# One core, deltanet and a multiplicative FFN: the hand-written list of 1706 steps put in another order

## The chip, the core and the metric

The kernel runs on one core of one Trainium2 chip. The metric is the device time of one execution in microseconds (us). TensorE is called PE here (its weight loads PEld), VectorE DVE, ScalarE ACT, GpSimd POOL and SyncE SP. SP issues every DMA of this kernel.

## The reference

Two blocks are joined. The first is a delta-rule recurrence over 768 positions for 4 batches of 8 heads, head size 48; the second multiplies two projections of its output and applies two further matrices:

```python
k_n = k / (np.linalg.norm(k, axis=-1, keepdims=True) + 1e-06)
for t in range(S):
    y[:, :, t] = np.einsum('bhd,bhde->bhe', q[:, :, t], state)
    v_old = np.einsum('bhde,bhd->bhe', state, kt)
    state = state + bt[..., None, None] * np.einsum('bhd,bhe->bhde', kt, vt - v_old)
...
a = x @ w1          # x: 3072 tokens x 384, from y
b = x @ w2          # w1, w2: 384 x 1024
h = a * b @ w3      # w3: 1024 x 1024
out = h @ w_out     # w_out: 1024 x 384
```

The four weights come as 64-bit floats; everything is computed in float32.

## The kernel before

The 768 positions are cut into 12 chunks of 64 (numbers 0 to 11), and two chunks make a pair (0 to 5). In a chunk the recurrence is solved in closed form, so that only a short chain runs from chunk to chunk. Two matrices are folded on the chip: w3·w_out becomes one matrix of 1024 x 384, so the second block is two products, an element-wise product and one more product. From pair 1 on, these products are done with fewer multiplications (sums of blocks on POOL and DVE, then 20 products per half instead of 24).

The work is written as generators, one for each part, and a **step** is what a generator does up to its next `yield`. The parts that matter below, by their letters in the list (a letter, then the chunk, pair or column block):

- `P`: one piece of a weight: a DMA into one of 5 `raw` buffers (L829), two activations on ACT (L837, L840), a shift on DVE (L842), an add on POOL (L844). `P0` to `P7` are w_out, `P8` to `P23` are w3 (two for each of 8 blocks of columns), `P24` to `P35` w1 and w2.
- `t`: four transposes of a w3 piece on PE (L880) and a copy out of PSUM (L204); `f`: one block of the fold in two halves of four products each on PE (L895), and a copy (L204).
- `k`, `q`, `v`, `p`: loads (L269, L280, L297; a `p` load is 8 DMAs). `K`, `Q` (chunks 0 and 1): transposes on PE (L404) and four copies (L204); `d` (the later chunks): four stream transposes on DVE (L390).
- `N`: norms of a pair, a chain of small DVE instructions. `s`: scores of a chunk on PE in two halves (L433, L439), each with a DVE product (L445) and an ACT copy (L457) with a POOL mask (L459).
- `u` (L492): copies that lay two chunks out for the inversion; `V`: the inversion of a pair on DVE, one transpose (L508) and 31 dependent pairs of instructions (L530 and L535, or L541 and L546).
- `e`: the corner of the inverse, copies (L589), a transpose on DVE (L599), and two sets of products on PE (L616) with ACT behind them (L641, L661).
- `c`: the chain of a chunk: three sets of products on PE (L687), each followed by one DVE instruction (L718, L727, L749) that the next set reads. `y`: the chunk's outputs on PE (L786), and copies on ACT (L805).
- `b`, `a`: the first products of pair 0 (L915). `m` (L1117): the products of a later pair, two halves `m10`, `m11` and so on, with adds on DVE (L1148), copies on ACT (L1145) and sums on POOL (L200). `S`, `G`, `W`, `T`: sums of blocks. `o` (L1199): the last products, `x`: results and stores.
- `warm+3` (L194): three products of 128x512 whose result nobody reads. `zp`, `zd`: memsets.

`ORDER` is a string of 1706 step names. The kernel calls the steps in that order, and `in_text_order` then ties every instruction to the one before it on its engine, so the string fixes the order of each of the five engines and of SP's DMA queue. Nothing is moved by a planner. A step's name can carry a mark: with `'`, what the step does by `put` (a copy out of PSUM) goes to the other of ACT and DVE, and what it does by `alone` (a sum of blocks) goes from POOL to DVE. Buffers are given out in turn as the steps are called: 5 `raw` buffers, 3 of `KQ`, 2 of `X`, 4 PSUM banks `ps_f`, 2 double banks `ps_w`, 10 slabs. An instruction waits where its inputs, or the last readers of the buffer it writes, are late; all behind it on its engine wait with it.

In order of time the list holds: loads, `K`, `Q` and scores of chunks 0 and 1 while the first weight pieces are converted; the inversion `V0` on DVE beside the folds on PE; corners and chains of chunks 0 and 1 with the last folds; the first products of pair 0 (`b`, `a`) beside the chunks 2 and 3; then four stages, from `oA0` to `oA4`, in each of which PE does the last products of one pair and the first products of the next, with the chain of two more chunks between them; and a tail of pair 5 alone.

Of the kernel before, what the change touches and what calls it, by code (L numbers as in the profile page):

```python
# [39 lines left out]
warm+3 P11 beta P2 P0 P11 P11 P11 P2 beta P3 k0 K0 P0 beta P0 P0 K0' K0 P6 P6 k1 K1 zd zd zd P2 g0 P2 P9 P3  # L40
q0 K0 K0 g0 g0 g0 g0 g0 P6 P9 g0 g0 K1 P9 P3 K1 P16 K1 q1 Q0 P10 Q0' N0 K1' P6 P16 P16 P3 Q0 Q0 Q0
P12 P13 P10 s0 N0 s0 P9 P5 s0 Q1 P10 P12 Q1' P16 zp zp P12 Q1' Q1 s0 Q1' P13 P8 p2 P5 P10 t3 s0 P13
P13 s0 s0 P1 P12 u0 u0 s1 s1 s1 s1 s1 s1 P7 P4 t2 t2' t3' u0 t5 t4 P5 t5' u1 u1 u1 V0 P8 P5 V0 P8 f1
P8 V0 t1 t1 t4 t0 t8 P17 d2 zp zp zp zp zp V0 V0 V0 V0 P14 k2 P1 P1 P1 t0 N0 t8 P4 P15 V0 P7 V0 V0
V0 P7 P17 V0 P4 V0 V0 V0 P17 P7 P4 P17 f2 f0 f2 f1 V0 s1 P14 d2 V0 V0 V0 k3 P14 P15 f2 V0 s0 g1 f0
f1 g1 P14 g1 t6 t9 P19 P18 P19 f0 t9 v0 V0 V0 g1 V0 P15 V0 P19 g1 P15 P19 zp t6 P18 P23 P22 v1 f4 f4
t7 t11 t7 V0 V0 V0 t11 g1 g1 P22 P23 f3 V0 P18 V0 V0 V0 V0 g1 P26 n0 P18 t10 V0 P23 V0 P22 V0 P20
t10 N1 n0 f3 P26 f5 f5 f3 e0 N1 e0 e0 e0 e0 p2 P20 P23 P22 d2 d2 P20 e1 e0 s2 f4 p3 P21 p3 P24 P25
e0 e0 P20 n1 t12 t15 P26 f5' s2 s2 d3 c0 c0 e1 t14 s2 e1 t14 t12 t15' P21 y0 s2 s2 d3 c0 f7 y0 P26
d3 P21 P21 d3 e1 u2 u2 u2 s1 n1 e1 c0 e1 s3 s3 s3 s3 s3 s3 y0 P27 t13 P29 c1 c1 t13' e1 P24 f6 u3 u3  # L50
u3 V1 V1 V1 V1 V1 P24 V1 V1 V1 P28 P24 e1 c1 c1 P25 P27 V1 P27 V1 P29 f7 p4 P32 y1 f7 f6 y1 P25 V1
V1 V1 V1 V1 V1 y1 P28 P25 P28 P27 b0 b0 v2 P30 P31 P28 f6 d4 V1 P29 P29 zp V1 V1 V1 P32 b3 b1 b2 b1
b3 b2 b7 d4 V1 V1 P32 V1 V1 V1 V1 b7 b4 a07 c1 a04 a07 a04 b4 a02 a00 a01 P30 a05 a02 V1 V1 V1 V1 V1
V1 V1 V1 V1 a00 n2 n2 P32 a01 P31 P30 P31 a05 a03 b5 e2 e2 e2 N1 a03 P31 P33 a06 c1 k4 p4 e2 P35 P34
k5 c2 P30 e2 d4 c2 P33 b5 d4 a00 b3 e3 g2 b3 p5 e2 a06 e2 P33 a00 g2 g2 g2 P33 b2 a03 e3 e2 P34 e3
c2 a03 c2 P35 P34 g2 P35 a02 a02 g2 b2 y2 b0 d5 e3 b0 d5 a01 g2 s4 P34 W y2 v3 P35 p5 g2 a01 N2 N2
b6 a06 b6 T T W T b6 b4 W a06 e3 n3 W s4 s4 s4 s4 d5 s4 d5 a04 e3 s4 b7 b6 b4 b7 s5 s5 s5 s5 s5 T s5
u4 v4 b5 a05 W W n3 n4 e3 s5 b5 a04 W' W S0 u5 V2 e3 c2 N2 V2 c2 V2 a07 c3 b1 a05 c3 b1 V2 V2 c3 c3
V2 a07 V2 V2 V2 V2 V2 oA0 V2 V2 y3 S0 S0' W W S0 S0 S0 n4 S0 xA0 oA0 oD0 W p6 S0 S0 S0 S0 y3 S0 S0
S0 y3 S0 xA0 oB0 oC0 V2 V2 V2 V2 V2 G1 V2 xB0 oB0 S0 G1 G1 G1 G1 c3 xA0 m10 d6 V2 V2 V2 V2 V2 xB0  # L60
xC0 oC0 xD0 m10 m10 G1 G1 G1' m10 m10 m10 m10 k6 d6 xC0 V2 V2 W xC0 V2 p6 V2 xD0 xC0 V2 W V2 m10 W
# [1341 lines left out]
```

## Time and profile before

| | |
|---|---|
| three runs | 546.81 us (median), 544.82 to 550.54 |
| profiled execution | 541.17 us, of which the core's span is 539.5 us |
| profiled execution below the median | 5.64 us, 1.0% |
| mean granted TensorE clock | 0.978 |
| PE, PEld busy | 513.8 us (95%), 431.6 us (80%) |
| DVE, ACT, POOL busy | 403.2 us, 221.5 us, 274.7 us |
| DMA | 52.66 MB, mean 98 GB/s |

In the profile's lists a row names source line, engine, operation and tiles (what is written `<-` what is read), its count, and then the busy time and the mean duration in ns. The chain of waits follows the end of the program back to what released each step.

### The profile page before, as it was taken

How to read it: one execution, taken by the hardware profiler on the slowest of the kernel's cores; microseconds unless marked ns; L12 is line 12 of the kernel's file. 1: busy time of each engine (PE TensorE's matmuls, PEld its weight loads, DVE VectorE, ACT ScalarE, POOL GpSimd, SP SyncE). 2: the span in 40 equal slices, each digit the busy share in tenths (PEclk: the TensorE clock that was granted, in tenths of full speed). 3: DMA queues.
4: the chain of work that ended last, by engine and by line, in shares of the span. 5: the costliest groups of instructions: out<-in, count | busy, mean ns of one | idle time of the engine just before them, and what ended most of it. 6: DMA issues, size and time to landing. Idle time of an engine off the chain costs nothing.

```text
span 539.5 us, 19915 instructions
## 1 busy us (share of the span) xinstructions
PE 513.8 (95%) x8466; PEld 431.6 (80%) x8466; DVE 403.2 (75%) x880; ACT 221.5 (41%) x453; POOL 274.7 (51%) x296
## 2 busy tenths in 40 slices
PE   6679998999999999999999999999999999999997
PEld 3555567688888988889988889878899788997886
DVE  2689986898667997869987799887879845536562
ACT  3787586747523133532134333245321342312210
POOL 4575763344889996066932258361368302051150
PEclk7599998999999999999999999999999999999999
DMA  8979974767554264654444561644314320010001
GB/s 222 239 202 237 239 112 114 154 163 151 98 84 81 60 139 65 104 108 78 103 102 61 82 114 49 137 80 56 53 52 108 76 40 4 17 51 8 2 1 60
DMA packets 197593, 52.66 MB, mean 98 GB/s; under 512 B 184576, under 2 KB 191872, under 8 KB 197504
## 3 DMA queue, kind: packets, MB, share of 16 engines
q1 hardware_dynamic: 197504, 51.38, 46.1%
q8 instruction: 67, 1.10, 0.9%
q14 instruction: 22, 0.18, 0.1%
HBM read 41.25 MB, written 8.91 MB: 93 GB/s over the span
## 4 chain that ended last, share of the span: by engine, by line
PE 65%; DVE 14%; SPq 7%; DMA 6%; ACT 3%; issue 3%; POOL 1%; DVEq 0%; ACTq 0%; POOLq 0%
PE ps_f L1117 26%; PE ps_f L1199 20%; PE ps_w L687 5%; SPq L297 4%; PE ps_f L895 3%; PE ps_w L786 3%; DVE tb L530 3%; DVE ps_w L535 3%; PE ps_f L915 2%; DVE KQ L390 2%; PE ps_w L616 2%; DMA raw<-in_moe_w_dram 2%; DMA perm<-in_q_dram 1%; PE ps_w L433 1%; SPq L269 1%
## 5 line engine op out<-in xcount | busy, mean ns | idle before, releaser
L200 POOL TENSOR_TENSOR ab<-ab 128x512 f32<-128x512 f32 (+1 forms) x57 | 65.5, 1167 | 67.5 <-DVE ab L1148 33.7
L1199 PE MATMUL ps_f<-w,ab 128*128 128x192 f32 x376 | 65.1, 327 | 0.0
L1117 PE MATMUL ps_f<-xT,w1s 128*128 128x256 f32 x240 | 63.4, 388 | 0.1
L1117 PE MATMUL ps_f<-xT,w2s 128*128 128x256 f32 x240 | 61.7, 387 | 1.4 <-DVE x_room L1148 1.0
L1199 PEld LDWEIGHTS ps_f<-w,ab 128*128 128x128 f32 x376 | 61.9, 190 | 0.7
L1148 DVE TENSOR_TENSOR ab<-ab,ps_f 128x512 f32<-128x512 f32 x70 | 47.6, 682 | 17.1 <-PE ps_f L1117 15.4
L1117 PEld LDWEIGHTS ps_f<-xT,w1s 128*128 128x128 f32 x240 | 43.5, 189 | 9.6 <-ACT x_room L1145 1.8
L1117 PEld LDWEIGHTS ps_f<-xT,w2s 128*128 128x128 f32 x240 | 43.6, 189 | 9.3 <-DVE x_room L1148 1.7
L459 POOL TENSOR_TENSOR PT<-PT,smask 128x512 f32<-128x512 f32 x20 | 25.4, 1276 | 44.9 <-ACT PT L457 44.7
L1199 PE MATMUL ps_f<-room,ab 128*128 128x192 f32 x272 | 47.2, 329 | 0.0
L546 DVE TENSOR_TENSOR ps_w<-ps_w,tb 128x31 f32<-128x31 f32 (+15 forms) x124 | 43.3, 349 | 4.5
L895 PE MATMUL ps_f<-w2s,w3T 128*128 128x384 f32 x128 | 43.8, 492 | 1.5 <-POOL w2s L844 1.0
L1199 PEld LDWEIGHTS ps_f<-room,ab 128*128 128x128 f32 x272 | 44.2, 190 | 0.5
L541 DVE TENSOR_TENSOR tb<-ps_w,Ub 128x31 f32<-128x31 f32 (+15 forms) x124 | 41.8, 337 | 3.4 <-DMA Ub<-Ud 0.3
L805 ACT COPY xT<-ps_w 48x256 f32<-48x256 f32 x96 | 30.6, 366 | 33.4 <-PE ps_w L786 32.9
L200 POOL TENSOR_TENSOR xT<-xT 128x256 f32<-128x256 f32 x44 | 31.9, 740 | 20.6 <-DVE xT L200 14.7
L1117 PE MATMUL ps_f<-xT,room 128*128 128x256 f32 x160 | 39.9, 381 | 0.0
L895 PEld LDWEIGHTS ps_f<-w2s,w3T 128*128 128x128 f32 x128 | 23.4, 190 | 17.3 <-POOL w2s L844 2.4
L1148 DVE TENSOR_TENSOR x_room<-x_room,ps_f 128x512 f32<-128x512 f32 x40 | 27.2, 679 | 11.1 <-PE ps_f L1117 10.0
L1145 ACT COPY x_room<-ps_f 128x512 f32<-128x512 f32 x20 | 11.7, 586 | 55.6 <-PE ps_f L1117 45.3
L1117 PEld LDWEIGHTS ps_f<-xT,room 128*128 128x128 f32 x160 | 30.1, 190 | 4.1
L1145 ACT COPY ab<-ps_f 128x512 f32<-128x512 f32 x20 | 11.7, 586 | 49.7 <-PE ps_f L1117 49.6
(196 smaller groups left out, 1078.5 us busy)
## 6 DMA issues: line engine op xcount, KB each, us to landing
raw<-in_moe_w_dram SPq DMA_DIRECT2D x16, 512.0 KB, 5.8
ktok<-in_k_dram SPq DMA_DIRECT2D x48, 96.0 KB, 3.4
vtok<-in_v_dram SPq DMA_DIRECT2D x24, 192.0 KB, 4.2
raw<-in_moe_w_dram SPq DMA_DIRECT2D x24, 192.0 KB, 4.3
out_dram<-osb SPq DMA_DIRECT2D x46, 96.0 KB, 1.7
raw<-in_moe_w_out_dram SPq DMA_DIRECT2D x8, 384.0 KB, 4.2
perm<-in_k_dram SPq DMA_DIRECT2D x40, 64.0 KB, 3.0
perm<-in_q_dram SPq DMA_DIRECT2D x32, 64.0 KB, 2.6
```

The source lines that it names most:

```text
L200: (dve if other else pool).tensor_tensor(out=out, in0=x, in1=y, op=op)
L297: sync.dma_start(out=dst[quarter(2 * e + j), :, :, tb, 0:nd].rearrange("t b a d -> t (b a) d"), in_=src.rearrange("b (a e) t d -> e (b a) ...
L459: pool.tensor_tensor(out=PT, in0=PT, in1=smask[:].unsqueeze(1).to_broadcast([P, H, C]), op=ALU.mult)
L541: dve.tensor_tensor(out=tv, in0=V[:, 0 : s + 1, s : s + 1].to_broadcast([P, s + 1, n]), in1=U[:, s, s + 1 : BS].unsqueeze(1).to_broadcast( ...
L546: dve.tensor_tensor(out=o, in0=o, in1=tv, op=ALU.subtract)
L687: pe.matmul(out(ps, r, h, z), lhsT=lhs(r, h, z), rhs=rhs(r, h, z), start=True, stop=True,)
L805: act.copy(out=xT[f, cc, p:NP:2, b : b + NR, :].rearrange("p a r t -> p r a t"), in_=pyv[f, z, b : b + NR],)
L895: pe.matmul(ps[:, 0:DM], lhsT=w3Ts[jc, kc // 4][:, kc % 4 * P : kc % 4 * P + P], rhs=wo[:, kc], start=(i == 0), stop=(i == KF - 1),)
L1117: pe.matmul(ps[:, n * g : n * g + n].rearrange("p (b c t) -> p b c t", b=HB, c=2), lhsT=product_weights(i, 2 * r + g), rhs=of[i], start=na ...
L1145: act.copy(out=t, in_=cell(what[1]))
L1148: dve.tensor_tensor(out=t, in0=t, in1=cell(what[2]), op=op)
L1199: pe.matmul(ps[b][:, b, :], lhsT=block(u, HF * f + i, z)[:, P * b : P * b + P], rhs=ws_[w][:, i], start=first and i == 0 and (b == 0 or n ...
```

## The change

The string `ORDER` is replaced as a whole by another order of the same steps. Of the marks, 55 steps carry `'` where 46 did; `warm+3` is there once in both. The program that results has the same instructions but for the engine of a few copies and sums: 12 of the 16 copies of `K` and `Q` are on ACT where 8 were, and some ten sums of blocks on DVE that were on POOL. Line numbers of the changed kernel are 47 higher, since the string is laid out in more lines. All else is the same text. The first lines of each string:

```diff
-warm+3 P11 beta P2 P0 P11 P11 P11 P2 beta P3 k0 K0 P0 beta P0 P0 K0' K0 P6 P6 k1 K1 zd zd zd P2 g0 P2 P9 P3
...
+P3 P3 P3 P3 zp zp zp zp zp zd k0 g0 g0 K0 K0 K0
+K0' K0 g0 zp zp zp g0 beta P9 zp P9 k1 zd g0 g0 g0
...
```

**The opening.** On SP, from the start of the program, before; `ktok0` and `ktok1` are chunks 0 and 1 of k, `X` is q, `raw` a weight piece:

```order
1 L829 DMA raw_115<-in_moe_w3_dram 128x1024
2 L1283 DMA xT0_78<-in_beta_dram 16x12x64 x2
3 L829 DMA raw_119<-in_moe_w_out_dram 128x768
4 L829 DMA raw_121<-in_moe_w_out_dram 128x768
5 L829 DMA raw_143<-in_moe_w_out_dram 128x768
6 L269 DMA ktok0_98<-in_k_dram 64x8x48 x4
7 L829 DMA raw_191<-in_moe_w_out_dram 128x768
8 L269 DMA ktok1_99<-in_k_dram 64x8x48 x4
9 L829 DMA raw_242<-in_moe_w3_dram 128x1024
10 L280 DMA X_246<-in_q_dram 64x16x48 x2
11 L829 DMA raw_269<-in_moe_w3_dram 128x1024
12 L280 DMA X_272<-in_q_dram 64x16x48 x2
```

The same queue now:

```order
1 L876 DMA raw_111<-in_moe_w_out_dram 128x768
2 L316 DMA ktok0_98<-in_k_dram 64x8x48 x4
3 L1330 DMA xT0_78<-in_beta_dram 16x12x64 x2
4 L876 DMA raw_178<-in_moe_w3_dram 128x1024
5 L316 DMA ktok1_99<-in_k_dram 64x8x48 x4
6 L876 DMA raw_195<-in_moe_w3_dram 128x1024
7 L327 DMA X_251<-in_q_dram 64x16x48 x2
8 L876 DMA raw_254<-in_moe_w3_dram 128x1024
9 L876 DMA raw_336<-in_moe_w3_dram 128x1024
10 L876 DMA raw_342<-in_moe_w3_dram 128x1024
11 L876 DMA raw_353<-in_moe_w3_dram 128x1024
12 L327 DMA X_421<-in_q_dram 64x16x48 x2
```

One weight piece instead of four stands ahead of the first load of k, and the first load of q moves up from place 10 to 7. On DVE, where the inversion `V0` begins (`Ub` is its transposed input, L508; `tb` its first pair; `w3T` are copies of transposed w3, the first of which the first fold reads; `w2s` holds pieces of w_out), before:

```order
45 L445 TENSOR_TENSOR U0_103<-ps_w_516,wt_376 128x512
46 L204 COPY w3T_551<-ps_f_546 128x512
47 L204 COPY w3T_553<-ps_f_448 128x512
48 L842 TENSOR_SCALAR w2s_108<-w2s_108 128x384
49 L204 COPY w3T_567<-ps_f_556 128x512
50 L508 STREAM_TRANSPOSE Ub_572<-xT1_79 128x1024
51 L842 TENSOR_SCALAR w3_574<-w3_574 128x512
52 L390 STREAM_TRANSPOSE KQ_609<-perm0_95 128x8x64
53 L530 TENSOR_TENSOR tb_616<-ps_w_578,Ub_572 128x31
```

The same place now:

```order
40 L889 TENSOR_SCALAR w3_513<-w3_513 128x512
41 L492 TENSOR_TENSOR U0_103<-ps_w_485,wt_321 128x512
42 L492 TENSOR_TENSOR U0_103<-ps_w_535,wt_321 128x512
43 L555 STREAM_TRANSPOSE Ub_572<-xT1_79 128x1024
44 L889 TENSOR_SCALAR w2s_108<-w2s_108 128x384 x2
45 L251 COPY w3T_600<-ps_f_577 128x512
46 L577 TENSOR_TENSOR tb_612<-ps_w_588,Ub_572 128x31
```

The three copies of `w3T` stood ahead of the inversion's transpose; now the last that the first fold needs stands behind it. `warm+3` is no longer PE's first work but stands between the last scores of chunk 1 and the last transposes ahead of the first fold.

**The corners and chains of chunks 0 and 1.** On ACT, before; L589 are the corners' copies, `late0` (L641) is what the second set of products of chunk 0's corner reads, `w34` a fold's result, `w3` and `raw` a weight piece:

```order
83 L589 COPY TT0_94<-Ub_572 128x16x32
84 L589 COPY TT0_94<-Ub_572 32x16x32
85 L837 ACTIVATE w3_977<-raw_883 128x512
86 L840 ACTIVATE raw_883<-raw_883 128x512
87 L589 COPY TT0_94<-Ub_572 128x16x32
88 L641 COPY late0_105<-ps_w_936 32x2x8x32 x2
89 L204 COPY w34_109<-ps_f_799 128x384
90 L661 ACTIVATE TT0_94<-ps_w_1042 32x2x8x32 x2
91 L589 COPY TT0_94<-Ub_572 32x16x32
```

And now:

```order
84 L636 COPY TT0_94<-Ub_572 128x16x32
85 L636 COPY TT0_94<-Ub_572 32x16x32
86 L636 COPY TT0_94<-Ub_572 128x16x32
87 L251 COPY w34_109<-ps_f_855 128x384
88 L884 ACTIVATE w3_990<-raw_869 128x512
89 L887 ACTIVATE raw_869<-raw_869 128x512
90 L636 COPY TT0_94<-Ub_572 32x16x32
91 L688 COPY late0_105<-ps_w_954 32x2x8x32 x2
92 L708 ACTIVATE TT0_94<-ps_w_1035 32x2x8x32 x2
```

The copy of a fold's result and the second L589 copy of chunk 1 now stand ahead of `late0`. On PE a little later, before (L895 is half a fold, L616 the first set of chunk 1's corner, L433 and L439 the scores of chunk 3, L687 the first set of chunk 1's chain):

```order
243 L895 MATMUL ps_f_1242<-w2s_108,w3T_1163 128x384 x4
244 L616 MATMUL ps_w_1269<-T110_104,U0_103 33x32 x32
245 L433 MATMUL ps_w_1306<-KQ_1094 64x128 x2
...
260 L439 MATMUL ps_w_1334<-KQ_1094 64x64 x4
261 L880 MATMUL ps_f_1372<-ident_83,w3_1169 128x128 x4
262 L687 MATMUL ps_w_1382<-S_1302,KQ_199 64x48 x32
263 L616 MATMUL ps_w_1418<-TT0_94,late0_105 33x32 x2
```

And now (L833 is chunk 0's output):

```order
243 L663 MATMUL ps_w_1213<-T110_104,U0_103 33x32 x32
244 L833 MATMUL ps_w_1254<-PT_390,X_1115 48x64 x32
245 L942 MATMUL ps_f_1311<-w2s_108,w3T_1117 128x384 x4
246 L734 MATMUL ps_w_1318<-S_1203,KQ_199 64x48 x32
247 L480 MATMUL ps_w_1352<-KQ_998 64x128 x2
...
262 L486 MATMUL ps_w_1380<-KQ_998 64x64 x4
263 L663 MATMUL ps_w_1415<-TT0_94,late0_105 33x32 x2
```

The chain's first set moved ahead of the scores of chunk 3, and now follows half a fold.

**A handover in the stage of pair 3.** On DVE, from the norms of pair 5 on, before; L390 are the transposes of chunk 11, L1148 the adds behind the products `m31`, L445 the scores of chunk 10, L749 the chain of chunk 8:

```order
683 L370 TENSOR_TENSOR wt_5579<-wt_5579,nt_5480 128x32
684 L1148 TENSOR_TENSOR ab_5260<-ab_5260,ps_f_5078 128x512
685 L1148 TENSOR_TENSOR late0_105<-late0_105,ps_f_5085 128x512
686 L390 STREAM_TRANSPOSE KQ_5594<-perm0_95 128x8x64 x2
687 L1148 TENSOR_TENSOR x_room0_97<-x_room0_97,ps_f_5159 128x512
688 L1148 TENSOR_TENSOR ab_5467<-ab_5467,ps_f_5085 128x512
689 L445 TENSOR_TENSOR U0_103<-ps_w_5613,wt_5579 128x512
690 L749 TENSOR_TENSOR S_5676<-S_5232,ps_w_5639 112x768
```

And now (L646 is the transpose of the corner of chunk 9):

```order
675 L417 TENSOR_TENSOR wt_5451<-wt_5451,nt_5429 128x32
676 L437 STREAM_TRANSPOSE KQ_5579<-perm0_95 128x8x64 x2
677 L1195 TENSOR_TENSOR ab_5332<-ab_5332,ps_f_5068 128x512
678 L1195 TENSOR_TENSOR late0_105<-late0_105,ps_f_5079 128x512
679 L796 TENSOR_TENSOR S_5592<-S_5211,ps_w_5464 112x768
680 L646 STREAM_TRANSPOSE T110_104<-TT0_94 128x512
681 L1195 TENSOR_TENSOR x_room0_97<-x_room0_97,ps_f_5124 128x512
```

The two transposes stand ahead of two adds of `m31` that they stood behind, and a chain step and a corner's transpose stand ahead of the third. On SP the loads of chunk 11's k (L297) stand ahead of the eight corner loads (L578) of chunk 9 that they stood behind.

More of the change, by code (lines that the diff above doesn't have):

```diff
@@ L45 @@
[L45 to L49, printed above, removed]
@@ L99 @@
+o5 x5 S5 S5' S5 S5' o5 x5 x5 S5 S5' o5 o5 x5 o5 o5
 x5 x5 x5 x5 x5 x5 x5 x5 x5 x5
```

156 lines of the change are left out of this document (103 added, 53 removed).

## The prediction

> **What bounds the kernel now.** I read the page first, then the busy times by stretch of time, then what PE waited for, then the chain of waits. The page says who is busy and which engine the chain of waits runs through:
>
> ```profile
> span 539.5 us, 19915 instructions
> PE 513.8 (95%) x8466; PEld 431.6 (80%) x8466; DVE 403.2 (75%) x880; ACT 221.5 (41%) x453; POOL 274.7 (51%) x296
> PE 65%; DVE 14%; SPq 7%; DMA 6%; ACT 3%; issue 3%; POOL 1%; DVEq 0%; ACTq 0%; POOLq 0%
> q8 instruction: 67, 1.10, 0.9%
> ```
>
> PE is busy 95% of the span. An order can only give back what PE does not use, so the question is where that lies. By stretch (length, then busy us and count of PE, PEld, DVE, ACT, POOL, then the granted clock):
>
> ```profile
> 8.00:28.50 20.50, 12.57 (x305) 10.53 (x306) 12.99 (x35) 10.78 (x23) 10.25 (x12) 0.50 1.01 242
> 28.50:37.00 8.50, 6.25 (x160) 5.13 (x159) 6.84 (x12) 7.91 (x13) 6.95 (x6) 1.00 0.75 162
> 37.00:75.00 38.00, 36.05 (x132) 21.13 (x133) 35.46 (x100) 28.43 (x53) 24.29 (x30) 1.00 0.90 203
> 75.00:108.50 33.50, 30.29 (x945) 23.15 (x945) 24.33 (x53) 24.28 (x45) 14.99 (x15) 0.95 0.67 139
> 108.50:168.40 59.90, 59.16 (x1153) 50.01 (x1151) 44.65 (x105) 30.51 (x67) 41.60 (x42) 1.00 0.64 125
> 168.40:460.00 291.60, 289.50 (x5257) 251.72 (x5251) 237.56 (x517) 100.43 (x219) 153.17 (x163) 1.00 0.41 78
> 460.00:539.50 79.50, 74.79 (x512) 67.41 (x510) 40.56 (x62) 15.30 (x32) 20.39 (x18) 1.00 0.07 24
> ```
>
> The reader is to see five limits. To 37 us PE waits for loads and for ACT, at half clock up to 28.5 us. From 37 to 75 us the folds fill PE (36.05 of 38.00) and the inversion fills DVE (35.46). From 75 to 108.5 us PE shows 30.29 busy of 33.50, with 945 small products. From 108.5 to 460 us PE idles only 0.74 and 2.10 us. The tail waits for its last results. What PE waited for in the whole run is short:
>
> ```profile
> PE ps_f L404 <- DMA ktok<-in_k_dram: 4.4, 4, 2.7
> PE ps_f L404 <- DMA X<-in_q_dram: 3.1, 2, 1.6
> PE ps_w L687 <- issue: 2.2, 2, 1.5
> PE ps_f L1117 <- DVE x_room L1148: 1.0, 2, 0.8
> PE ps_f L895 <- POOL w2s L844: 1.0, 2, 0.7
> PE ps_f L880 <- POOL w L844: 0.8, 2, 0.6
> ```
>
> The Trainium skill, in "Perfetto Trace Analysis", section "Identifying the Most-Contended Engine", calls the matmuls' busy share a bad measure and asks for the weight loads' share; here that is 80% against 95%. So a stretch with PE "busy" can still be slow, and I look at the pace of its products below.
>
> **Term A, the opening up to 75 us: +1.0.** The rows for it are the instructions around 37 us, and the durations of what ACT and DVE do ahead of it:
>
> ```profile
> 37.04 2.20 PE L895 MATMUL ps_f<-w2s,w3T 128*128 128x384 f32 x6 [0.53 <-DVE w3T L204]
> 38.73 0.67 ACT L837 ACTIVATE w<-raw 128x512 f32<-128x512 f32 x1
> 38.87 1.25 DVE L508 STREAM_TRANSPOSE Ub<-xT 128x1024 f32<-128x1024 f32 x1 [0.36 <-POOL xT L492]
> raw<-in_moe_w_out_dram SPq DMA_DIRECT2D x8, 384.0 KB, 4.2
> L837 ACT ACTIVATE w<-raw 128x512 f32<-128x512 f32 x16 | 10.9, 681 | 7.5 <-DMA raw<-in_moe_w_dram 4.8 <-PE ps_f L895 2.6
> L840 ACT ACTIVATE raw<-raw 128x384 uint32<-128x384 uint32 x8 | 4.4, 545 | 0.0
> L204 ACT COPY KQ<-ps_f 48x512 f32<-48x512 f32 x8 | 4.6, 580 | 4.5 <-PE ps_f L404 4.3
> L492 ACT COPY xT<-U 96x512 f32<-96x512 f32 x4 | 4.3, 1084 | 1.0 <-DVE U L445 1.0
> L842 DVE TENSOR_SCALAR w2s<-w2s 128x384 uint32<-128x384 uint32 x8 | 4.0, 497 | 0.9 <-ACT w2s L837 0.9
> L204 DVE COPY w3T<-ps_f 128x512 f32<-128x512 f32 x5 | 3.3, 681 | 0.0
> ```
>
> Before, the first fold starts at 37.04 us; the last `u1` copy on ACT ends at 38.73 us, and DVE's transpose of V0 follows. Up to that copy's end ACT does 12 conversions of 128x512 (0.68 us), 10 of 128x384 (0.545), 8 copies of K and Q (0.58), 3 of PT (the same price), 4 of L492 (1.09) and 0.8 us of small ones: 25.1 us. After, it is 14, 6, 12, 3 and 4, two copies of w3T at KQ's price and 1.4 us of small ones: 28.4 us, 3.3 more. But it starts sooner and waits less. Before, ACT's first conversion starts at about 4 us, so some 9.5 us until 38.73 were waiting. The two loads that PE waited 4.4 + 3.1 us for now stand ahead of all but one to three weight pieces, so I leave 9.5 - 7.5 = 2.0 us. The first piece is issued first, at 0.8 us, and takes 4.2 to land: 5.0 + 28.4 + 2.0 = 35.4 us, so V0 begins 3.4 us sooner. The first fold, though, now stands behind V0's transpose on DVE: 1.25, two shifts of 0.497, the copy of 0.681, and three handovers of about 0.2: 35.4 + 3.5 = 38.9 us, 1.9 later. Behind it PE has the same 36.05 us of folds and transposes, and two waits for pieces (1.0 and 0.8) that a later start shortens; I give back half of them, 0.9. So A = +1.0, at 75 us. Bounds: with no waiting on ACT and both piece waits gone, -1.0; with 9.5 us of waiting kept, the start moves 7.5 us, +8.5. I stay near the lower end because the loads' places in the queue are sure. Twelve copies of K and Q on ACT instead of 8 free 4 x 0.68 us of DVE, which waits there anyway: nothing. The sums that move from POOL to DVE (about ten) lie where DVE idles 54 us of 291.6: nothing by themselves; their lateness is in term D.
>
> **Term B, 75 to 108.5 us: -1.5.** Here the chain has stops named issue, in which PE waits for nothing that the profile shows:
>
> ```profile
> 80.29 1.51 issue
> 84.34 0.57 issue
> 90.98 0.32 issue
> 94.58 0.67 issue
> 255.60 1.06 PE ps_w L687 x57
> 81.80:95.25 13.45, 12.21 (x382) 0.87 0.48 118
> L204 ACT COPY w<-ps_f 128x384 f32<-128x384 f32 x7 | 3.3, 477 | 1.8 <-PE ps_f L895 1.8
> L589 ACT COPY TT<-Ub 32x512 f32<-32x512 f32 x4 | 4.4, 1094 | 0.0
> ```
>
> Between the stops at 80.29 and 94.58 PE does 382 products in 13.45 us, 35 ns each; elsewhere 57 of the same small kind take 1.06 us, 19 ns each. PE's 2 x 8466 instructions over 67 fetched packets make 253 a packet: blocks of instructions are used up in the small products faster than they come. After, the first set of chunk 1's chain stands behind half a fold, whose four products use up 8 instructions, and no longer behind 48 products of scores; the last three stops (1.56 us) should go. Against it, on ACT the copy behind `late0` and a corner's copy move ahead of it: 0.477 + 1.094 = 1.57 us, and PE's next set of the corner waits for it; the first stop (1.51) lies within that wait, so +0.06 is left. B = -1.5. Bounds: all four stops gone and the copies hidden, -3.1; stops kept beside the copies, +1.6. The Trainium skill, in "Runtime: NRT & Kernel Launch", section "Instruction fetch mechanics", has PE's instructions come in 16 KiB blocks of 256 and a crossing mostly hidden. The packets agree (1.10 MB over 67 is 16.4 KB), the stops do not. By that rule the stops have another cause and stay, B would be +0.1 and the sum +2.6.
>
> **Term C, 108.5 to 168.4 us: 0.** PE idles 0.74 us there; the first products of pair 0 cover the chain in both orders.
>
> **Term D, the four stages to 460 us: +1.5.** A set of the chain or an add of `m` on DVE (0.682) is late for PE when PE's own work since its releaser is shorter:
>
> ```profile
> L1148 DVE TENSOR_TENSOR ab<-ab,ps_f 128x512 f32<-128x512 f32 x70 | 47.6, 682 | 17.1 <-PE ps_f L1117 15.4
> 377.37 3.07 DMA perm<-in_q_dram
> 382.71 0.33 PE L433 MATMUL ps_w<-KQ 48*64 48x128 f32 x2 [0.36 <-ACT PT L457]
> ```
>
> With these rows' durations laid along both orders, I count 13 handovers in the first three stages that are short by over 0.3 us before, and 25 after (an estimate by hand: chunk 6's corner to its chain, chunk 9's likewise, chunk 8's corner, and in the stage of pair 3 the transposes of chunk 11 ahead of two adds of m31). PE's idle time before is 2.10 us, 0.16 for each of the 13. Twelve more at 0.16: +1.9. Against it, chunk 11's k is now loaded ahead of chunk 9's corner; the 0.36 us that PE waits at 382.7 behind its late transfer should go. D = +1.5. Bounds: every one of the twelve costs a whole DVE add, +8.2; all of the 2.10 goes, -2.1. I take the low price because most of the 13 cost nothing now.
>
> **Term E, the tail: 0.** Three sums move to DVE, which is idle half of it.
>
> **Sum**: +1.0 - 1.5 + 0 + 1.5 + 0 = +1.0. The profiled execution took 541.17 us (span 539.5 and 1.7 around it), so it would take 542.2; the median of the runs is 546.81, so 547.8 on its scale. About 1% is what a measurement of this kernel can tell from no change.
>
> **The rivals.**
> - Faster: the opening's loads leave ACT without waits (A at -1.0), the fold hides the blocks (B at -3.1), and the earlier transfers take all of PE's idle time in the stages (D at -2.1): -6.2, 540.6 us. For it: V0 begins sooner, and three stops stand in the chain. Against: 28.4 us of ACT work, and 25 short handovers for 13.
> - Slower: the DVE handovers of stages 1 to 3 cost what they are short by. Place: DVE, ahead of the adds of `m`, above all chunk 11's transposes, which must wait for the outputs of chunk 8 to leave their KQ buffer. Price: 12 x 0.682 = 8.2 for 1.9, so +7.3, 554.1 us. It decides from about 0.55 us each. Against: 0.16 each now.
> - The clock: PE's unread products have left the start, and the folds begin at half clock. Before, half clock held from 8.0 to 28.5 us with PE 61% busy, full clock came with 74%. Two halves of a fold twice as slow: by the row below 8 products of 0.32 us, +2.6, so 550.4 us. For it, less work at the very start; against, the three unread products (2.42 us with a fourth) now stand straight ahead of the folds.
>
> ```profile
> 67.30 7.74 PE ps_f L895 x24
> 3.52 2.42 PE L194 MATMUL ps_f<-ident 128*128 128x512 f32 x4
> ```
>
> The Trainium skill, in "TensorE: Matmul & The Clock Gate", Part 1, says that half rate is the default and that one busy window of about 3.4 us releases it; the rows agree, and by it the clock rival needs the scores ahead of the folds to leave such a window unfilled.
>
> **How the numbers follow.** The forecast's case 0.42, faster 0.27, slower 0.25, the clock 0.06. The forecast's own range, from the lower bounds of A and B to half of D's upper, is 541.5 to 553.5. It passes 1% on both sides a little, 0.03 each. So faster by over 1% is 0.27 + 0.03 = 0.30, within 1% 0.36 + 0.06 = 0.42, slower 0.25 + 0.03 = 0.28. For 8 in 10 the range takes in both rivals: 538.5 to 557.0.
>
> **What would show it.** A: V0's transpose near 35.5 us, the first fold near 39, the corner of chunk 0 on PE near 76. B: no stop between the scores of chunk 3 and the chain of chunk 1, the first product of pair 0 near 108 us; `late0`'s copy 1.6 us behind its products. D: PE's idle time from the first `oA` to the last 3.6 us for 2.10, with L1148 as the releaser. The prediction is wrong if the opening waits for a `raw` buffer that POOL still holds, behind the masks, so that a piece of w_out comes late for the second half of a fold; or if a late transfer of the stages now stops DVE with adds of `m` queued behind it.

## The result, and the profile after

| | before | after |
|---|---|---|
| median of 20 runs each, us | 546.46 (541.78 to 553.28) | 549.55 (546.17 to 554.87) |
| ratio | | 1.0072, 95% interval 1.0049 to 1.0095 |
| profiled execution, us | 541.17 | 549.02 |
| the same against its kernel's median | 5.3 below | 0.5 below |

The new order is 0.7% slower, within the 1% that the prediction called no change, but on the slow side of it. The medians are of all 20 runs; the ratio leaves out the few slow ones. The last row matters for all that follows: the two profiles differ by 7.85 us, the medians by 3.1. The profile of before is one of its quick executions, so a comparison stretch by stretch overstates the loss by 4.8 us.

The page of after, the same four lines:

```profile
span 547.0 us, 19911 instructions
PE 513.9 (94%) x8466; PEld 432.7 (79%) x8466; DVE 406.1 (74%) x885; ACT 223.8 (41%) x457; POOL 265.8 (49%) x287
PE 78%; DVE 7%; ACT 5%; SPq 4%; issue 3%; DMA 2%; ACTq 0%; DVEq 0%
q8 instruction: 66, 1.08, 0.8%
```

PE's busy time is the same to 0.1 us (513.8 and 513.9), so that in sum the difference is time in which PE did nothing; products slowed by half clock, which count as busy, are in both profiles. By stretch, with the marks of before (length, then busy us and count of PE, PEld, DVE, ACT, POOL, then the granted clock):

```profile
28.50:37.00 8.50, 7.42 (x129) 5.01 (x122) 6.26 (x10) 8.29 (x16) 7.26 (x7) 1.00 0.82 202
37.00:75.00 38.00, 34.55 (x124) 20.78 (x122) 33.63 (x99) 26.48 (x50) 22.48 (x22) 1.00 0.85 198
75.00:108.50 33.50, 28.36 (x883) 20.50 (x882) 23.88 (x48) 23.27 (x40) 16.46 (x18) 1.00 0.77 152
108.50:168.40 59.90, 58.47 (x1103) 49.52 (x1104) 44.23 (x107) 29.60 (x68) 40.17 (x40) 1.00 0.65 110
168.40:460.00 291.60, 286.48 (x5112) 248.77 (x5105) 238.77 (x525) 99.09 (x213) 141.39 (x154) 0.99 0.42 80
```

PE idles 1.93 us more between 75 and 108.5 us (30.29 busy before, 28.36 now), 0.69 more up to 168.4 and 3.02 more in the stages. What PE waited for, longest first but for the rows left out:

```profile
PE ps_f L451 <- DMA ktok<-in_k_dram: 9.1, 5, 4.7
PE ps_f L942 <- DVE w3T L251: 3.1, 1, 3.1
PE ps_w L734 <- issue: 1.9, 1, 1.9
...
PE ps_f L1164 <- DVE ab L1195: 1.2, 2, 0.9
PE ps_f L927 <- issue: 1.2, 1, 1.2
PE ps_f L942 <- issue: 1.1, 1, 1.1
PE ps_f L1164 <- DVE x_room L1195: 0.9, 2, 0.8
...
PE ps_w L480 <- DVE vtok L765: 0.6, 1, 0.6
```

To place the loss I worked out, for each profile, the time at which the same amount of PE's work is done (every product counted with the mean duration of its kind), and took that of before's profile off. I call it the lag. In us, at marks of before's time (75 is the end of the folds, 108.5 the first product of pair 0, 168 the last work ahead of the stages, 535 the end):

```
kernel            75   108.5    168    190    228    389    535
after           +0.3   +1.7   +4.1   +5.9   +7.0   +8.1   +7.6
x_swap_after    +3.7   +5.6   +7.6   +8.5   +9.7  +11.3  +11.1
x_fill_after    +1.9   +4.2   +6.3   +6.4   +7.6   +8.1   +7.6
x_warm_after    -0.1   +0.7   +1.6   +1.6   +2.8   +4.4   +3.9
x_three_after   +0.8   +1.7   +3.7   +3.8   +5.0   +5.2   +6.4
x_spread_after  +1.8   +3.9   +3.7   +4.0   +5.2   +6.4   +6.4
x_swap_before   +0.8   +0.4   +5.7   +5.6   +9.4  +10.8  +10.8
```

The lower rows are experiments told below; the last is a variant of before. So after loses +0.3 up to 75 us, +1.4 up to 108.5, +2.4 up to 168, +1.8 more up to 190, and +1.7 from there to the end. How a kind of product is weighted moves single entries by some tenths, those at 228 by up to 0.8 us.

The greatest single loss lies at the start of the stages. The chain of waits of after, at the first set of chunk 3's chain (L734):

```profile
168.36 0.84 PE ps_w L734 x55
169.21 1.88 issue
171.09 0.33 PE ps_w L734 x7
```

And the timeline of PE right behind it:

```profile
171.35 4.44 PE L1246 MATMUL ps_f<-w,ab 128*128 128x192 f32 x16
175.58 2.91 PE L1246 MATMUL ps_f<-room,ab 128*128 128x192 f32 x16
```

PE stops for 1.88 us in the middle of 64 small products, and the chain names no other engine as what it waits for. Then 16 products take 4.44 us where the next 16 of the same kind take 2.91. PE's busy time and granted clock (the column behind the count) by single microseconds say why:

```profile
173.00:174.00 1.00, 1.00 (x5) 0.50 0.50 62
174.00:175.00 1.00, 1.00 (x5) 0.50 0.36 35
176.00:177.00 1.00, 1.00 (x8) 1.00 0.76 133
```

The clock was halved, 3.4 us long from 172.5 on by the trace's record of it. Stop and half clock together cost 1.88 + 1.53 = 3.4 us.

### The profile page after: what moved, and what is told of

Same layout as the page of the kernel before. It is cut to its first block, busy times and chain, and to the rows that moved or that the text cites. A ratio compares the mean times of both kernels' runs of the same rounds, so it can differ in the third digit from the quotient of the medians.

```text
span 547.0 us, 19911 instructions
## 1 busy us (share of the span) xinstructions
PE 513.9 (94%) x8466; PEld 432.7 (79%) x8466; DVE 406.1 (74%) x885; ACT 223.8 (41%) x457; POOL 265.8 (49%) x287
## 3 DMA queue, kind: packets, MB, share of 16 engines
q8 instruction: 66, 1.08, 0.8%
## 4 chain that ended last, share of the span: by engine, by line
PE 78%; DVE 7%; ACT 5%; SPq 4%; issue 3%; DMA 2%; ACTq 0%; DVEq 0%
PE ps_f L1164 32%; PE ps_f L1246 20%; PE ps_w L734 7%; PE ps_w L833 5%; PE ps_f L962 5%; PE ps_w L663 2%; SPq L344 2%; PE ps_f L942 2%; PE ps_w L480 2%; DVE ps_w L582 2%; DVE tb L577 2%; PE ps_w L486 2%; SPq L876 1%; DMA ktok<-in_k_dram 1%; SPq L316 1%
## 5 line engine op out<-in xcount | busy, mean ns | idle before, releaser
L247 POOL TENSOR_TENSOR ab<-ab 128x512 f32<-128x512 f32 (+1 forms) x56 | 63.2, 1149 | 78.1 <-DVE ab L1195 31.5
L1246 PE MATMUL ps_f<-w,ab 128*128 128x192 f32 x376 | 67.0, 333 | 0.0
L1246 PEld LDWEIGHTS ps_f<-w,ab 128*128 128x128 f32 x376 | 63.0, 193 | 0.9 <-issue 0.3
L1195 DVE TENSOR_TENSOR ab<-ab,ps_f 128x512 f32<-128x512 f32 x70 | 47.7, 683 | 21.5 <-PE ps_f L1164 20.5
L1246 PE MATMUL ps_f<-room,ab 128*128 128x192 f32 x272 | 47.5, 328 | 0.0
L852 ACT COPY xT<-ps_w 48x256 f32<-48x256 f32 x96 | 30.6, 366 | 39.5 <-PE ps_w L833 38.3
L1246 PEld LDWEIGHTS ps_f<-room,ab 128*128 128x128 f32 x272 | 44.7, 191 | 0.4
L1195 DVE TENSOR_TENSOR x_room<-x_room,ps_f 128x512 f32<-128x512 f32 x40 | 27.2, 681 | 12.3 <-PE ps_f L1164 11.9
L247 POOL TENSOR_TENSOR xT<-xT 128x256 f32<-128x256 f32 x38 | 27.4, 736 | 13.7 <-DMA xT<-xT 6.6
L247 POOL TENSOR_TENSOR ab<-ab,x_room 128x512 f32<-128x512 f32 x8 | 10.3, 1290 | 44.4 <-DVE x_room L1195 44.4
```

Source lines behind the costliest of these rows:

```text
L247: (dve if other else pool).tensor_tensor(out=out, in0=x, in1=y, op=op)
L852: act.copy(out=xT[f, cc, p:NP:2, b : b + NR, :].rearrange("p a r t -> p r a t"), in_=pyv[f, z, b : b + NR],)
L1195: dve.tensor_tensor(out=t, in0=t, in1=cell(what[2]), op=op)
L1246: pe.matmul(ps[b][:, b, :], lhsT=block(u, HF * f + i, z)[:, P * b : P * b + P], rhs=ws_[w][:, i], start=first and i == 0 and (b == 0 or n ...
```

## The experiments

Theory 1: the loss comes from PE's instruction stream. Small products use its blocks up faster than new ones come; the new order packs them more densely ahead of chunk 3's chain; and a stop brings a stretch of half clock. Theory 2, the rival: the loss is in the handovers from DVE to PE in the stages, and the stops cost what they cost before. Theory 3 came later: the loss is due to the marks, which put sums on DVE instead of POOL. The names of steps are those of the list; all ratios are to before, timed beside the kernel. Counts of products are the profile's, which shows two for each that the program issues (x32 in the order is x64 here). Each experiment renumbers the source lines: L692 and L693 are L734 of after, L1204 and L1205 are L1246, and the other lines, too, stand about 42 lower than in after.

**x_swap_after.** After, with a product of column block 5 moved from ahead of the corner to between it and the chain's products:

```diff
-c2 c2 a05 a05 e3 e3 a07 c3 c3
+c2 c2 e3 e3 a07 a05 c3 a05 c3
```

> The changed order with one step moved: the second product of a05 (six products of pair 0, 1.5 us on PE) stands between the second set of chunk 3's corner's predecessor and chunk 3's chain (behind e3.6, ahead of c3.0) and no longer ahead of both. Theory 1 (PE runs out of instruction blocks at c3.0, 1.88 us, and that stop halves the clock for a window of 3.4 us, 1.7 us more): the stop at 169 us goes or shrinks under 0.5 us, no half-clock window follows it, and the time falls by about 3.6 us against the changed kernel, so about 1.000 of the kernel before. Theory 2 (late handovers on DVE in the stages cost the time): nothing changes here, 1.007 of the kernel before.

548.92 us, 1.0095 (1.0056 to 1.0135). The chain of waits shows that the stop has stayed, after the 57th product (in after's timeline, too, 57 stand ahead of it):

```profile
171.07 1.00 PE ps_w L692 x57
172.07 1.76 issue
173.83 0.46 PE ps_w L692 x7
```

A miss for the expectation, and a hint: the same instructions had been issued up to there, only in another order, so a block edge would lie in the same place.

**x_fill_after.** After, with three unread products of 128x512 ahead of chunk 3's first set. They are added work: the timeline shows 2.84 us for them.

```diff
-c3
+c3+3
...
             ps = two_banks()
+            fill(ps[:, 0])
```

> The changed order with three products of 128x512 more, whose result nobody reads, ahead of c3.0: about 1.8 us of work added on PE. Theory 1: the block comes while they run, the stop of 1.88 us and the half-clock window go, and the added work costs nothing or less than nothing: 0 to -1.8 us against the changed kernel, 1.003 to 1.007 of the kernel before. Theory 2: the added work is paid in full, +1.8 us, 1.010 of the kernel before.

547.78 us, 1.0054 (1.0023 to 1.0085). PE by stretch: no stop and full clock.

```profile
169.00:174.00 5.00, 5.00 (x138) 1.00 0.66 153
174.00:178.00 4.00, 4.00 (x26) 1.00 0.53 72
```

With 2.8 us more work on PE the kernel is not slower than after, since the stop and the half clock (3.4 us) are gone; the lag from 168 to 190 us falls from 1.8 to 0.1. This speaks for theory 1; by theory 2 the added work had to show.

**x_swap_before.** Before, with the corner's last sets moved to stand straight ahead of chunk 3's chain:

```diff
-a07 c3 b1 a05 c3
+a07 e3 e3 c3 b1 a05 c3
```

> The kernel before with the same place made dense: e3.6 stands straight ahead of c3.0, and a07.2 no longer between them. Theory 1: a stop named issue of 1 to 2 us appears inside c3.0 near 166 us, perhaps with a half-clock window behind it: +1 to +3.6 us, 1.002 to 1.007 of the kernel before. Theory 2: the same work in the same stage, 1.000.

545.53 us, 1.0022 (0.9987 to 1.0056): no difference shown. It doesn't tell what it was made for, since the wait that arose there was for ACT:

```profile
PE ps_w L692 <- ACT TT L666: 1.4, 1, 1.4
```

**x_mid_only.** Before, with the steps between the corner of chunk 0 and the first `oA` in the changed order:

```diff
-P20 e1 e0 s2 f4 p3 P21 p3 P24
+P20 d3 P20 e1 e0 s1 s2 P22 s2 s2 e0
...
```

> The kernel before, with the changed order for the steps between chunk 0's corner (75 us) and the first last products (168 us) alone. Theory 1: the corners' stretch costs about 1.4 us and the stop with its window 3.7 us, as in the changed kernel, so nearly the whole loss: 1.006 to 1.009 of the kernel before. Theory 2: the loss lies in the stages behind, so within 0.003 of the kernel before. A third theory, the opening: also none of the loss.

555.45 us, 1.0194 (1.0141 to 1.0247), more than the whole change. PE waited 4.1 us in three stops in L692 alone, against 2.2 in two in before:

```profile
PE ps_w L692 <- issue: 4.1, 3, 2.1
```

Two halves of two orders make a third one, with its own block edges and its own turn of the buffers. The pieces don't add up, and this split proves nothing on its own.

**x_warm_after.** After, with the three unread products moved to stand directly ahead of the first fold:

```diff
-P7 warm+3 V0 P2 P5 t2
+P7 V0 P2 P5 t2
...
-t8 t5 V0 V0
+t8 t5 warm+3 V0 V0
```

> The changed order with the three unread products (warm+3) moved behind the last transposes ahead of the first fold, into the 3.1 us in which PE waits there for a copy on DVE. Theory 1 (a wait of that length lets the clock fall to half for one or two windows of 3.4 us while the folds run, as two of three profiles of this order showed, and the folds are PE's own bound): no half-clock window between 38 and 50 us, the mean granted clock of the runs rises by one window (0.003), and the time falls by 1 to 2 us against the changed kernel: 1.004 to 1.006 of the kernel before. Theory 2 (the stages' handovers on DVE): the same time as the changed kernel, 1.007.

547.80 us, 1.0088 (1.0048 to 1.0128). The profiled execution has no half clock at all from the folds on and took 543.4 us in span, but the 12 runs don't follow it: the gain expected isn't there. Whether a window of half clock falls near the folds changes from one profile of this opening to the next (none to 6.8 us of it between 36 and 47 us), and the position of three products alone doesn't decide it: x_three_after, with them in the same place, has such a window from 36.6 to 40.0 us.

**x_three_after.** After, with the edits of x_warm_after and x_fill_after, and chunk 11's transposes moved back behind adds of `m31`:

```diff
-p11 d11 d11 m31 m31 m31 m31 m31 m31
+p11 m31 m31 m31 d11 d11 m31 m31 m31
```

> The changed order with three repairs: the unread products moved as in the run beside it, three more unread products ahead of chunk 3's chain (1.8 us of work on PE), and the transposes of chunk 11 behind the adds of m31 that they stood ahead of. Theory 1: the half-clock window in the folds (1.7 us or more), the stop of 1.9 us with its window (1.7) and the wait of 0.93 us at 379 us go, 1.8 us are added: about -4 us against the changed kernel, 1.000 of the kernel before. Theory 2: only the 0.9 us go and 1.8 are added, 1.009.

547.00 us, 1.0074 (1.0041 to 1.0107): no ratio of 1.000, so a miss; the interval takes in theory 2's 1.009. The added products take 2.84 us, not the 1.8 expected. But the trace tells what the handover costs. DVE in after, then PE in after:

```profile
378.06 1.30 DVE L437 STREAM_TRANSPOSE KQ<-perm 128x512 f32<-128x512 f32 x2 [1.86 <-PE ps_w L833]
379.29 0.65 DVE L1195 TENSOR_TENSOR ab<-ab,ps_f 128x512 f32<-128x512 f32 x1
```

```profile
377.93 1.13 PE L1164 MATMUL ps_f<-xT,w_room 128*128 128x256 f32 x4
379.99 1.13 PE L1164 MATMUL ps_f<-xT,w1s 128*128 128x256 f32 x4 [0.93 <-DVE ab L1195]
```

PE in x_three_after, the same products:

```profile
376.03 1.13 PE L1123 MATMUL ps_f<-xT,w_room 128*128 128x256 f32 x4
377.00 1.03 PE L1123 MATMUL ps_f<-xT,w1s 128*128 128x256 f32 x4
```

In after, the transposes wait 1.86 us for the outputs of chunk 8 to leave their buffer, the add waits for the transposes, and PE 0.93 us for the add. Moved back, the wait is gone, and the lag between 365 and 389 us grows by 0.5 where it grows by 1.5 in after. What was won there went into the added products and into a new stop of 0.83 us at 465 us.

**x_pace.** Before, with 512 unread products of 64x64 by 64x48, all into one place of PSUM, ahead of chunk 3's first set, to measure how fast small products can be fed:

```diff
+            for _ in range(128 * unread[0]):
+                pe.matmul(ps[half(0), 0, 0:D], lhsT=ident[half(0), 0:C], rhs=ident[half(0), 0:D], start=True, stop=True)
```

> The kernel before with 512 unread products of 64x64 by 64x48 ahead of chunk 3's chain: 1024 instructions, four blocks of 256. Theory 1 (blocks come no faster than about 4.4 us each, 35 ns a product): they take 16 to 18 us, with stops named issue of 1 to 2 us between dense runs at 19 ns a product. Rival (blocks are fetched ahead and hidden; the stops have another cause): 9.5 us, no stops.

652.78 us, one run. The group of these products:

```profile
L690 PE MATMUL ps_w<-ident 64*64 64x48 f32 x1024 | 106.2, 298 | 0.0
```

106.2 us over 1024 is 104 ns each, at half clock but for the start, although the profile counts PE as busy all that time; 64 of the chain's products, into different places, take 1.15 us at full clock in x_spread_after, 18 ns each. It failed as a measure of blocks.

**x_late_only.** Before up to the first `oA`, the changed order from there:

```diff
-oA0 V2 V2 y3 S0 S0' W W
+oA0 S0 S0 W' oD0 W W W W
...
```

> The kernel before up to the first last products (168 us), and the changed order from there on. Theory 1: the stages and the tail cost 1 to 2 us (0.9 of it at the transposes of chunk 11), 1.002 to 1.004 of the kernel before. Theory 2 (the twelve more short handovers on DVE carry the loss): 1.006 to 1.010.

The 12 runs fall into two groups, four between 542.07 and 549.80 us and eight between 557 and 562; the ratio of the first is 1.0058 (0.9994 to 1.0122), which takes in both theories. The only profile is of the second kind and shows where its time went. On DVE:

```profile
173.85 14.60 DVE L205 TENSOR_TENSOR room<-w2s,w1s 128x512 f32<-128x512 f32 x1
```

On POOL, the longest piece of an unbroken row, nearly all sums, that begins before 173.65 us:

```profile
179.13 5.52 POOL L205 TENSOR_TENSOR ab<-ab 128x256 f32<-128x256 f32 x8
```

The same sum takes 0.685 us in after, where POOL stands idle beside it. Here it ends at 188.5 us, after POOL's row has had its first gap, at 187.9 us, and PE waits 11.9 us for it. That this wait is what sets the eight long runs apart is a guess, since no run of the other group was profiled. From 190 us on this profile's lag grows by 2.6 us to the end, against 1.7 in after.

**x_pace2.** Before, with the 64 products of chunk 3's first set issued nine times over (the same results written again):

```diff
-            for r in range(NR):
+            for r in [r for _ in range(1 + unread[0]) for r in range(NR)]:
```

> The kernel before with the 64 products of chunk 3's first chain set issued nine times instead of once (the same operands, the same result): 512 small products more in one dense run, 1024 instructions, four blocks of 256. Theory 1 (blocks of instructions come no faster than one in about 4.4 us): the 576 products take about 18 to 20 us with stops of 1 to 2.5 us, about one for each 128 products. Rival (instructions are always there; the stops of these kernels are something else): 576 x 19 ns = 10.9 us without a stop.

559.95 us, one run. The timeline of PE:

```profile
170.34 2.08 PE L692 MATMUL ps_w<-S,KQ 48*64 48x48 f32 x128 [1.92 <-issue]
174.07 7.14 PE L692 MATMUL ps_w<-S,KQ 48*64 48x48 f32 x257 [1.65 <-issue]
```

Between two stops stand exactly 128 products, with their weight loads 256 instructions. From one stop's end to the next it is 174.07 - 170.34 = 3.73 us, of which 2.08 are work. Then the clock halves, 257 products take 7.14 us (28 ns each, 3.6 us for 128), and there is no stop any more. The nine sets take 16.0 us (165.25 to 181.21) with two stops: less than theory 1 expected, more than the rival. Nor is the pace fixed: where two stops one block apart follow each other, 3.7 to 5.2 us lie between their ends, in this profile and in those of before, x_late_only, x_fill_after and x_spread_after.

What settles the cause of the stops is the trace's record of the queue q8. Each of its packets is one block of 16 KB, and their count fits PE's instructions (67 packets before, 70 here with 512 products more). Of the 45 stops named issue of over 0.5 us in the fourteen profiles, 43 end 2.2 to 3.2 us after such a fetch began and 1.2 to 2.0 us after it landed (the other two are in x_mid_only). In after, the fetch for the stop at 169.21 us begins at 168.73, takes 0.96 us, and PE goes on at 171.09. So PE waited for its next block of instructions. The Trainium skill, in "Runtime: NRT & Kernel Launch", section "Instruction fetch mechanics", gives blocks of 16 KiB or 256 instructions, which agrees; that a crossing is mostly hidden does not hold at these stops of 1.92 and 1.65 us.

**x_spread_after.** After, with a product of column block 3 (six large products) moved to between chunk 3's corner and its chain:

```diff
-a07 v4 a03 a03 V2 n3 W c2 c2 a05 a05 e3 e3 a07 c3 c3
+a07 v4 V2 n3 W c2 c2 a05 a05 e3 e3 a07 a03 c3 a03 c3
```

> The changed order with one step moved: the second product of a03 (six products, 1.5 us) stands between chunk 3's corner and its chain, while a05's stays ahead of the corner, so that two such products lie in the block of instructions that runs from c2.4 to c3.0 instead of one. Theory 1: that block lasts 4.5 us instead of 3.1, the stop at c3.0 (1.9, 1.1 and 1.8 us in three profiles) shrinks under 0.5 us and no half-clock window follows: -1.5 to -3 us against the changed kernel, 1.002 to 1.005 of the kernel before. Theory 2 (the stages): 1.007.

547.43 us, 1.0045 (1.0012 to 1.0078). PE's timeline:

```profile
168.34 1.56 PE L920 MATMUL ps_f<-xT,w2s 128*128 128x256 f32 x6
169.83 1.15 PE L692 MATMUL ps_w<-S,KQ 48*64 48x48 f32 x64
170.91 2.87 PE L1204 MATMUL ps_f<-w,ab 128*128 128x192 f32 x16
```

The 64 products run through in 1.15 us and the 16 behind them at full clock (2.87 for 4.44), with no work added. In its profile the lag from 108.5 to 190 us is +0.1 where after has +4.2. The median ratio falls from 1.0072 to 1.0045; the two intervals overlap, so the gain over after is shown by the trace and only pointed to by the times.

The stop went for another reason than I had expected. The block's edge moved with the product, so that its 128 products take 3.35 us (167.34 to 170.69), hardly more than the 3.24 in after (165.97 to 169.21). But the fetch of the next block begins at 167.90 us, 2.8 us before PE reaches the edge; in after, and in x_swap_after with six large products in the same place, it begins only 0.5 us before. What decides when a fetch begins no run here shows.

**x_marks_after.** After, with the marks on sums, copies and adds (`G`, `W`, `S`, `m`) as before has them, 43 changed:

```diff
-m11 m11' m11 S1' u7
+m11 m11 m11 S1 u7
...
```

> The changed order, with the marks of G, W, S and m steps as in the kernel before, so that the same sums as before run on DVE and on POOL. Theory 3 (sums of two SBUF operands on DVE are held up while POOL's own sums run, as one of 14.6 us was in the run with the late part alone, and a dozen more of them cost PE in the stages): 1 to 3 us less than the changed kernel, 1.002 to 1.005. Theory 1: nothing at the stop; 1.005 to 1.008.

553.75 us, 1.0187 (1.0129 to 1.0245): theory 3 falls, the old marks make the new order worse, and theory 1's 1.005 to 1.008 is missed as well. A new wait for DVE in the stages, one of three:

```profile
PE ps_f L1122 <- DVE late L1153: 1.2, 1, 1.2
```

**x_before_fold.** Before, with the second half of a fold between the corner and the scores of chunk 2, to remove the 1.51 us stop there:

```diff
-f5 f5 f3 e0
+f5 f3 e0
...
-e1 e0 s2 f4
+e1 e0 f5 s2 f4
```

> The kernel before with one step moved: the second half of the fold f5 (four products, 1.4 us) from ahead of chunk 0's corner to between its two sets of products, ahead of the scores of chunk 2. Theory 1: the half fold covers the wait for the copy of late0 and gives the next block of instructions 1.4 us more, so the stop in c0.0 (1.5, 1.9, 1.8 and 1.3 us in four profiles of this order) shrinks by about that, and the half-clock window behind it goes in most executions: -1.5 to -3 us, 0.995 to 0.997 of the kernel before. Rival (the corner is bound by ACT and DVE, PE's stop is slack): 1.000 to 1.002.

547.49 us, 1.0027 (0.9981 to 1.0073): no difference shown, and not the gain expected. That stop is gone, but the fold had hidden DVE's transpose of the corner:

```profile
PE ps_w L621 <- DVE T L604: 2.3, 1, 2.3
```

Half clock followed, and the moved fold's eight products took 4.54 us. No version that I ran beats the kernel before.

## Why the prediction was right, and where it was wrong

The sum came out too low: +1.0 us forecast, +3.1 measured between the medians (0.72%, 3.9 us, by the ratio). Sign and size class are right, in good part by luck: of the terms only D came as worked out, B had the wrong sign, C was put at 0, and between the two profiles the terms add up to 7.6 us, which is more than 1%. Two figures of the prediction do not follow from its own terms either. A's lower bound of -1.0 gives back only half of the two piece waits (with both gone it is -1.9). And the own range of 541.5 to 553.5 is wider than what it is said to be made of: A and B at their lower bounds give 544.2, half of D's upper bound 550.4.

**Term A, the opening: +1.0 forecast, +0.3 measured in after's profile.** The sum holds, its parts less so. V0's transpose was forecast near 35.4 us and the first fold near 38.9. DVE first, then PE:

```profile
38.53 1.25 DVE L555 STREAM_TRANSPOSE Ub<-xT 128x1024 f32<-128x1024 f32 x1 [2.72 <-POOL xT L539]
```

```profile
40.94 1.24 PE L942 MATMUL ps_f<-w2s,w3T 128*128 128x384 f32 x3 [3.14 <-DVE w3T L251]
```

The transpose came 3.1 us later than forecast, and the fold 2.0. The term that was mis-sized is ACT's waiting. I had taken all 7.5 us that PE waited for k and q off it, which left 2.0. The load of k did land sooner: PE's first transposes of k start at 4.67 us (9.59 before), and the 9.1 us in the row above are long because PE has no other work from the program's start. But between its first conversion, at 4.13 us, and the end of the last `u1` copy, at 38.3, ACT stood idle for 8.2 us (11.6 in before, where I had taken 9.5), 4.6 of them ahead of one copy of K. Its work was 26.0 us where I had counted 28.4. The late fold was evened out by work that PE had done ahead of the fold: from 28.5 to 37 us it is busy 1.17 us more than in before (7.42 for 6.25), from 37 to 75 us 1.50 less (34.55 for 36.05), which leaves the 0.3. My sum had no term for that. The corner of chunk 0 then starts on PE at 75.6 us, near the 76 forecast. In other profiles of the same opening the lag at 75 us goes from -0.1 to +3.7, with the half clock in the folds.

**Term B, 75 to 108.5 us: -1.5 forecast, +1.4 measured. Wrong in sign.** The step that failed is "the last three stops (1.56 us) should go", since half a fold uses up only 8 instructions. The chain of waits of after:

```profile
81.22 0.70 PE ps_f L927 x5
81.92 1.23 issue
...
89.28 1.55 PE ps_f L942 x4
90.83 1.08 issue
91.91 1.56 PE ps_f L942 x4
93.47 1.12 PE ps_w L734 x64
95.05 0.97 DVE vtok L765
```

The stops moved: 1.23 and 1.08 us here and two shorter ones, where before had 3.07 us in four. One lies inside transposes, one inside the very fold that was to hide it, between its fourth and fifth product: a large product doesn't prevent a stop when the small ones ahead of it have used up the block. What counts is where the edge of 256 instructions falls and when the fetch of the next block began, not what stands next to the chain. The copy behind `late0`, priced at 1.57 us against the first stop, came 0.4 us behind its products and not 1.6; PE waited 1.0 us for ACT at the chain (0.3 before). And there is a wait that I had not priced: chunk 1's chain now holds one of the two double banks until DVE has read it (L765), and the scores of chunk 3, moved behind it, wait 0.6 us for that bank. In six of the seven profiles of the changed order this stretch costs +0.8 to +2.3 us; the seventh, x_marks_after, has -1.0 here. Before's profile has a window of half clock in this stretch (83.1 to 86.5 us) and after's has none, so the loss would else have been larger. The first product of pair 0 came at 110.3 us (108 forecast).

**Term C, 108.5 to 168.4 us: 0 forecast. Wrong.** Its step, "the first products of pair 0 cover the chain in both orders", held for the chain's waits but not for PE's instruction stream: the corner and the chain of chunk 3 now follow each other as 128 small products in a row, and the next block comes late. The stop cost 1.88 us and the half clock behind it 1.53, and x_spread_after removes both. That is 3.4 of the 4.2 us of lag between 108.5 and 190 us; 0.4 more is another stop, ahead of the scores at 159.9 us, and the rest I did not place. I had used the blocks in term B only, as a thing to be won, and did not look for a place where the new order makes a stop.

**Term D, the stages: +1.5 forecast; from 190 us to the end +1.7 measured,** 1.2 to 2.6 in the other profiles with these marks. The engine and the size are right. PE's idle time from the first `oA` on is 3.4 us in after by the row below (3.6 forecast, 2.10 before), with L1195, the L1148 of before, as the releaser of 1.3 (of the 2.1 in the rows above, 0.8 lies in the tail):

```profile
171.30:468.00 296.70, 293.34 (x5325) 0.99 0.41 77
```

The price was unevenly spread, however: few of the 25 short handovers cost anything, and two places carry most: chunk 11's transposes (0.93 us, shown by x_three_after) and, between 215 and 228 us of before, two adds of `m11` for which PE's weight loads wait 0.71 and 0.47 us and PE itself 0.3. Every profile of the changed order with its own marks loses time there, 0.5 to 1.2 us by how the products are weighted. The first of the two, on PE's loads:

```profile
231.17 0.73 PEld L1164 LDWEIGHTS ps_f<-xT,w1s 128*128 128x128 f32 x4 [0.71 <-DVE ab L1195]
```

Here DVE was late with the norms of a pair ahead of the add. The count times a mean of 0.16 gave the right sum from the wrong picture.

**Term E, the tail: 0.** The lag changes by -0.5 from 389 us to the end, so nothing is lost there.

The terms measured in the profile sum to 0.3 + 1.4 + 4.2 + 1.7 = 7.6 us; the two spans differ by 7.5. That the medians differ by 3.1 means that before's ordinary execution loses some 4.8 us that its profiled one does not. x_swap_before shows a loss of this kind, its lag growing from 5.6 to 9.4 us between 190 and 228 in a stage that its edit left alone: PE waits 2.3 us there for a corner's transpose on DVE, which a late load holds up. Half clock is another part: the 80 runs of before that were timed beside the experiments have a median granted clock of 0.975 against the profile's 0.978; that is about one window of 3.4 us more at half clock, by estimate 1.7 us. How the rest is spread over the terms stays open.

**The rivals.** Faster fell with B: of its three gains none came. Slower by the DVE handovers needed 0.55 us each at twelve places; one place reached it clearly (0.93), the next on PE has 0.31. The clock rival named a mechanism that did come. In after's profile half clock missed the folds and came behind a stop, at 172.5 us; but in four of the seven profiles of this opening (x_swap_after, x_fill_after, x_spread_after, x_marks_after) one or two windows of it lie in the folds, between 40.6 and 47.4 us, and the lag at 75 us is 1.8 to 3.7 us there. So the +0.3 of term A is a favourable profile, too. The Trainium skill, in "TensorE: Matmul & The Clock Gate", Part 1, lets the rate fall back after an idle window of about 3.4 us; here a stop of 1.88 us was enough, so the measurement decides against a wholly idle window as the condition. Not every stop does it: behind one of 1.78 us, at 92 us in x_spread_after, full clock held.

## What to carry to other kernels

Where many small products follow each other, count PE's instructions, weight loads included, in blocks of 256, and look in the trace for when each next block is fetched: PE went on 2.2 to 3.2 us after the fetch began, so one that begins 0.5 us before PE reaches the edge ends in a stop, and the stop may halve the clock behind it. A block that is used up in 3.2 us is in danger, but not lost: x_spread_after's took 3.35 us without a stop. A large product next to the chain is no remedy by itself (x_swap_after); whether it brings the fetch forward has to be tried. And before summing differences stretch by stretch, set each profiled execution against the median of its own runs: here 4.8 of 7.6 us were the luck of one profile.

## What the runs showed of the hardware that I had not expected

- PE's instructions come in blocks of 256, and the trace records the fetch of each: 0.96 us for the 16 KB in after at 168.73 us, and 1.39 us more until PE went on. In x_pace2 two stops ended 3.73 us apart with 256 instructions between them; at half clock, when 128 products took 3.6 us, there was none.
- A sum on DVE with both inputs in SBUF stood 14.6 us behind unbroken sums on POOL, in the one profile of x_late_only. The Trainium skill, in "GPSIMD Engine Reference", section "1. Specifications", says that POOL shares its SBUF interfaces with DVE and names DVE instructions with two SBUF inputs; the trace agrees with that, and the hold ended just behind POOL's first gap. That POOL's row of sums was the cause was not tested by a run that breaks it up.
- Products of 64x48 into one place of PSUM took 104 ns each in x_pace, most of them at half clock; products of 48x48 into different places took 28 ns each at half clock in x_pace2. They differ in shape and operands as well, so the place is not shown to be the cause. In x_pace half clock lasted 105.8 us, with PE counted as busy throughout.
